# Linear attention and a low-rank mixer on one core: part of one batch's first product by Strassen's algorithm, one cast shared by two engines, a weight load gated later

## The chip, the cores and the metric

One core of a Trainium2 chip runs the whole program. The metric is the device time of one execution in microseconds (us); lower is better. The kernel before took 290.35 us (median of 3 runs, 290.05 to 291.34).

The engines are called as the profile calls them: PE (matrix products), PEld (its weight loads), DVE and ACT (elementwise work), POOL (elementwise work, and issue of one kind of DMA), SP (issue of the other kind). DMAs that POOL issues run in the queue that the profile names q0 software_dynamic, those of SP in q1 hardware_dynamic; both are served by the same 16 DMA engines.

## The reference

There are 8 batches, 8 heads, 576 positions, head width 64, model width 512. First comes attention without softmax, then a mixer:

```python
phi(x) = concat(relu(x) * cos_w, relu(x) * sin_w)        # 64 -> 128 features
kv  = einsum('bhsf,bhsd->bhfd', phi(k), v)
num = einsum('bhsf,bhfd->bhsd', phi(q), kv)
den = einsum('bhsf,bhf->bhs', phi(q), sum_s phi(k)) + 1e-6
x   = num / den                                          # as [8, 576, 512]
u   = x + (x^T @ U @ V)^T                                # U [576, 32], V [32, 576]
out = u + relu(u @ w_ch1) @ w_ch2                        # 512 -> 2048 -> 512
```

All inputs and the output are float32; the kernel computes in bf16 with float32 sums.

## The kernel before

**Tiling.** A batch's 576 positions are four blocks of 128 and a tail of 64; the tails of two batches share one block. A batch's first product (u times w1, 2048 hidden columns) is laid out in 16 blocks `j` of 128 hidden columns; plain, each block takes four matmuls of 128x512 (`g1_main`, L702 to L719) and an eviction with relu on ACT (L717). The second product (hidden times w2) gives the batch's 512 output columns.

**Strassen.** In batches 3 to 6 (`MIXED`, L815) half of the first product's blocks go by Strassen's algorithm: for `m` in (0, 2), the blocks 4m to 4m+3 take seven parts of four 128x256 matmuls each (`g1_part`, L620; matmuls L653), and the blocks 4m+4 to 4m+7, named s4 to s7, are plain ones laid between the parts. The parts need sums and differences of blocks of w1 (`w1_form`, tile `sa`, DVE, L591) and of u^T (`uT_form`, tile `tb`, DVE, L608). Parts 1, 6, 5 and 3 add up one after the other in one bank of PSUM (`al_ps`) and ACT reads it after each (L114 to tile `pw`, or L687); parts 2, 7 and 4 go to banks called `be_ps`, and DVE adds the `pw` copy to each (L678). Part 4 adds onto part 7's bank, after DVE has read that. The relu of these blocks is made by DVE (L675), or for the batches in `RELU_A` by ACT two slots later (L670). The second product of batches 1 to 7 goes by Strassen as a whole (`w_part`, matmuls L892, sums of hidden blocks by `hid_form`, L857).

**Order.** The order of all work is written out by hand. A list of slots holds PE's units in order, batch after batch; `todo` and `beside` hang other work (loads, casts, the attention of a later batch) on slot numbers, and each engine runs its instructions in the order in which they were written. In a slot, PE's own unit comes first, then what hangs on it. `starts[b]` is the slot at which batch b's first product begins; starts[2] is slot 70. The tail's second product of the first pair (`g2_tail`, L796) is in the slots 66 to 69.

**The start.** SP loads q, k and v of batch 0 (v in four DMAs: two for heads 0 to 3, two for heads 4 to 7; L74 and L80). DVE and ACT make the features of q and k, PE the transposes of q and the sums over k. Then `first_chain` (L1269) makes batch 0's x: v is cast to bf16 (tile `v0`, DVE, L116: heads 0 and 1, heads 2 and 3, then heads 4 to 7 in one instruction); the product of k and v is made for heads 0 to 3 (L353) and for heads 4 to 7 (`kv_unit`, L341); the reciprocals of the denominators (`rec`, L429 and L430) and the normalisation (L1240, DVE, nine instructions, and L1263, ACT) follow, then u^T and the first product. POOL loads w1 in four quarters and w2 in four quarters (L102, L108). Each of these loads waits for a mark: a one-element copy by POOL that reads something which must be done first. The first quarter of w1 waits for `q_tl` (L1352), its other quarters for `q_tlT` (L1358), w2 for the transposed q of batch 1 (L1380). In the same way SP's loads of batch 1 stand behind small DMAs that read `k_p` (L1354) and `z_sb` (L1361).

**Banks of PSUM.** `G3` is three banks that are used in turn, `T1` one bank, `OA` and `OB` one each, which are there only from slot starts[3] - 2 on.

**SP in the steady state.** SP issues the loads of the next batch and the transposes of q (`qtr_dma`, L408 and L413) and of u (`utr_dma`, L535 and L541), in order; each waits in SP's queue for its data. Batch 7's transposes of q stand ahead of batch 6's transposes of u.

Of the kernel before, what the change touches and what calls it, by code (L numbers as in the profile page):

```python
# [10 lines left out]
FP32 = mybir.dt.float32  # L11
# [6 lines left out]
def kernel(  # L18
# [11 lines left out]
    nc = tc.nc  # L30

    B = 8
    H = 8
# [3 lines left out]
    P = 128  # L37
    DM = 512
# [207 lines left out]
    X1S = ("x", 1)  # L246
# [20 lines left out]
    def bank(shape, dt, tag, bufs, name):  # L267
        if tag == "x":
            return ps.tile([P, 2, 512], FP32, tag="X", bufs=1, name=name)[:, 0, 0 : shape[1]]
        if tag in ("oA", "oB"):  # L270
            return ps_rest[1].tile(shape, dt, tag=tag, bufs=bufs, name=name)
        if tag == "O":
            t = ps_rest[2].tile([P, 2, 512], FP32, tag=tag, bufs=bufs, name=name)
            return t if len(shape) == 3 else t[:, 0, 0 : shape[1]]
        return ps.tile(shape, dt, tag=tag, bufs=bufs, name=name)
# [331 lines left out]
        )[n]  # L607
        V_.tensor_tensor(out=t[:, n], in0=a, in1=b_, op=ALU.subtract)  # L608

    RELU_A = (4, 6)  # L610
    relus = []

    def late_relus():
# [6 lines left out]
    def g1_part(b, m, part):  # L620
        if b not in hid:
            hid[b] = pool.tile([P, NJ, 512], BF16, tag="hid", bufs=1, name="hid")
        last = b == B - 1
        if b not in pw:
            pw[b] = [
                pool.tile([P, 3, 512], FP32, tag=tag, bufs=1, name="pw")
                for tag in ("pw", "k_p")[: 1 + last]
            ]
        ks = slice(2 * m, 2 * m + 2)

        def s_of(n):
            return sa[m % 2][:, m // 2, n]

        lhs, rhs = {
            1: lambda: (w1_block(0, 0, ks), uT_block(b, 0, 0)),
            2: lambda: (w1_block(0, 1, ks), uT_block(b, 1, 0)),
            3: lambda: (s_of(3), uT_block(b, 1, 1)),
            4: lambda: (w1_block(1, 1, ks), tb[b][:, 3]),
            5: lambda: (s_of(0), tb[b][:, 0]),
            6: lambda: (s_of(1), tb[b][:, 1]),  # L640
            7: lambda: (s_of(2), tb[b][:, 2]),
        }[part]()
        if part == 1:
            g_al[b, m] = bank([P, DM], FP32, *((OA, OB, T1)[m % 3] if last else T1), "al_ps")
        elif part in (2, 7):
            tg = (X1S, G3) if last else (G3, OA)
            g_be[b, m, part] = bank([P, DM], FP32, *tg[part == 7], "be_ps")
        t = g_al[b, m] if part in (1, 3, 5, 6) else g_be[b, m, 2 if part == 2 else 7]
        opens = part in (1, 2, 7)
        res = t.rearrange("p (k n) -> p k n", k=2)  # L650
        for k_ in range(2):
            for d in range(2):
                nc.tensor.matmul(  # L653
                    out=res[:, k_, :], lhsT=lhs[:, d, k_, :], rhs=rhs[:, d, :],
                    start=(opens and k_ == 0 and d == 0), stop=(k_ == 1 and d == 1),
                    skip_group_check=not opens,
                )
        p_, w_, y_ = (
            pw[b][m % 2 if last else 0][:, i].rearrange("p (k n) -> p k n", k=2)
            for i in range(3)  # L660
        )

        def block(i, r):
            return hid_block(b, i, r, ks)

        def relu(o):
            if b in RELU_A:
                relus.append([
                    2,
                    lambda: nc.scalar.activation(  # L670
                        out=o, in_=o, func=AF.Relu, bias=0.0, scale=1.0
                    ),
                ])
                return
            V_.tensor_scalar(out=o, in0=o, scalar1=0.0, scalar2=None, op0=ALU.max)  # L675

        def add(o, x):
            V_.tensor_tensor(out=o, in0=x, in1=res, op=ALU.add)  # L678

        if part == 1:  # L680
            cast(A_, p_, res)
        elif part == 6:
            cast(A_, w_, res)
        elif part == 5:
            cast(A_, y_, res)
        elif part == 3:
            nc.scalar.activation(  # L687
                out=block(0, 1), in_=res, func=AF.Relu, bias=0.0, scale=1.0
            )
        elif part == 2:  # L690
            add(block(0, 0), p_)
            relu(block(0, 0))
        elif part == 7:
            add(block(1, 1), y_)
            relu(block(1, 1))
        else:
            add(block(1, 0), w_)
            relu(block(1, 0))
# [96 lines left out]

    def g2_tail(pr, part):  # L796
        if part == 0:
            o_ps[pr] = bank([P, DM], FP32, *(OB if pr else T1), "ot_ps")
        o = o_ps[pr]
        for j in range(part * 4, part * 4 + 4):  # L800
            nc.tensor.matmul(  # L801
                out=o, lhsT=hid_tl[pr][:, j, :], rhs=w2_bf[:, j, :],
                start=(j == 0), stop=(j == NJ - 1),
            )
        if part < 3:
            return
        o_s = pool.tile([P, DM], FP32, tag="o_tl", bufs=1, name="o_tl")
        nc.vector.tensor_tensor(out=o_s, in0=u_tl[pr], in1=o, op=ALU.add)
        for i in range(2):
            store_eng(2 * pr).dma_start(  # L810
                out=out[2 * pr + i].rearrange("(m k) n -> m k n", k=9)[:, 4],
                in_=o_s[i * TS : i * TS + TS, :],
            )

    MIXED = {3: (0, 2), 4: (0, 2), 5: (0, 2), 6: (0, 2)}  # L815
    FULL = [b for b, ms in MIXED.items() if 2 in ms]
    HD = DM // 2
    KB = NJ // 2
# [223 lines left out]
    def lay(units, in_second):  # L1042
        slots.extend(units)
        second.extend([in_second] * len(units))

    HALF = ("1", "s4", "6 2", "s5", "5 7", "s6", "3", "s7 4")

    def first_units(b):
        starts[b] = len(slots)

        def unit(names, m):
            def go():
                for n in names:
                    if n[0] == "s":
                        g1_main(b, 4 * m + int(n[1]))
                    else:
                        g1_part(b, m, int(n))

            return go

        for m in (0, 2):
            if m in MIXED.get(b, ()):
                lay([unit(n.split(), m) for n in HALF], False)
            else:
                lay([lambda j=j: g1_main(b, j) for j in range(4 * m, 4 * m + 8)], False)
        for i in range(4 * (0 < b)):
            n = 12 + 2 * i if b == 1 else (9, 11, 17, 18)[i] if b in MIXED else 8 + i
            beside.setdefault(starts[b] + n, []).append(
                lambda i=i: hid_form(b, (1, 2, 4, 3)[i], 0)
            )  # L1070
# [58 lines left out]
    def attention_plan(b):  # L1129
# [22 lines left out]
        else:  # L1152
# [6 lines left out]
                        put(F + s_, feature, *ops.pop(0), eng)  # L1159
            V0 = starts[b - 2] + 9 if b > 3 else F + 1  # L1160
            at_q, at_load = (F + 7, F + 8, F + 8) if late else (F + 5, F + 7, F + 7), (F + 8, F + (16 if late else 14), V0 + (8 if late else 5))
            if b == 6:
                at_q, at_load = (F + 7, F + 12, F + 12), (F + 12, F + 16, V0 + 8)
            if b == 3:
# [7 lines left out]
            if late:  # L1172
                kv_at, x_at = G + 3, [G + i for i in (5, 8, 13, 16, 18)]
            elif b - 1 in FULL:
                kv_at, x_at = G + 1, [G + i for i in ODDX]
            elif b - 1 in MIXED:
                kv_at, x_at = G + 1, [G + i for i in X5]
            a_at = x_at[4] + (3 if b in (4, 6) else 2)
            u_at = a_at + 1
# [89 lines left out]
    def first_chain(b, xz, z, v_ps):  # L1269
# [9 lines left out]
        cast(V_, v0[:, 0:2], vst[:, 0:2])  # L1279
        cast(V_, z_sb, z[:, :, 0])  # L1280
        cast(V_, v0[:, 2:4], vst[:, 2:4])
        cast(V_, v0[:, 4:H], vst[:, 4:H])
        qtr_evac(b, 4, A_, t_q[4])
        kv_sb[b] = pool.tile([P, H, E], BF16, tag="kv", bufs=2, name="kv")
        acc = bank([P, 4, D], FP32, *G3, "kv_ps")
# [2 lines left out]
        kv0_mm(b, acc, (2, 3))  # L1288
        cast(A_, V_bf, v_ps.rearrange("r (c p) -> r c p", c=4))
        cast(A_, kv_sb[b][:, 0:4, 0:D], acc)  # L1290
        den_mm(b, d, (3, 4))
        recip(rec, d[:, :, :, 0])
        x0 = [xh_mm(b, c, 0, *G3) for c in ORD[0:2]]
# [55 lines left out]
        z_mm(0, c, z)  # L1349
    qtr_evac(0, 3, A_, t_q[3])  # L1350

    G_.tensor_copy(out=mark[0:1], in_=q_tl[0:1, 0, 0:1])  # L1352
    w1_load(0)
    nc.sync.dma_start(out=mark2, in_=k_p[0][0:1, 0, 0, 0:1])  # L1354
    load_odd(qst, q, 1)
    load_even(qst, q, 1)
    first_chain(0, xz, z, v_ps)
# [77 lines left out]
    def put(at, thunk):  # L1435
        todo.setdefault(at, []).append(thunk)
# [2 lines left out]
    s6 = starts[B - 2]  # L1439
    for n in range(4):  # L1440
        for m in (0, 2):
            put(starts[2] + (-4, -3, -1, 1)[n], lambda n=n, m=m: w1_form(n, m))
            put(
                (s6 + (1, 2, 3, 4)[n], starts[B - 1] + (-3, -1, 1, 3)[n])[m // 2],
                lambda n=n, m=m: w1_form(n, m + 1),
            )
        for b in MIXED:
            put(starts[b] + (-3, -2, 0, 2)[n], lambda b=b, n=n: uT_form(b, n))
        put(starts[B - 1] + (-2, -1, 0, 2)[n], lambda n=n: uT_form(B - 1, n))
        put(starts[B - 1] + len(LAST) + 5 + 2 * n, lambda n=n: tl_form(n))  # L1450
# [43 lines left out]
```

## Time and profile before

| what | value |
|---|---|
| median of 3 runs | 290.35 us (290.05 to 291.34) |
| the profiled execution's own time | 290.51 us |
| its span (first to last instruction) | 288.7 us |
| PE busy | 98% of the span, 3110 matmuls |
| DVE, ACT, POOL busy | 76%, 61%, 25% of the span |
| DMA | 53.32 MB, 185 GB/s over the span |
| granted clock of PE | 0.999 |

The span is the time from the first to the last instruction in the trace; the own time of the same execution is 1.8 us longer. Times inside the trace count from the span's start. A matmul's record in the trace is longer than the distance to the next one, since matmuls are pipelined: a group of four 128x512 is recorded as 1.03 us and holds PE for 0.86.

### The profile page before, as it was taken

Reading aid. Unit: us, or ns where it says so; the run is one execution under the profiler, and the core shown is the slowest. Engines: PE = TensorE matmul, PEld = TensorE weight load, DVE = VectorE, ACT = ScalarE, POOL = GpSimd, SP = SyncE. Lnnn points to the kernel's source line nnn. Section 1 sums busy time; section 2 is a strip of 40 time slices with the busy share of each in tenths; the row PEclk is TensorE's granted clock in tenths of the full one; section 3 lists DMA queues with packets and bytes.
Section 4 is the critical chain, followed back from the end, with each engine's and each line's share of the span. In section 5 each row is a group of like instructions: output and inputs, shape, how many; then the busy total and the mean of one; then the engine's idle time right before and its main releaser. Section 6 shows DMA issues by size and latency. Waiting matters only on the chain.

```text
span 288.7 us, 7553 instructions
## 1 busy us (share of the span) xinstructions
PE 283.0 (98%) x3110; PEld 209.6 (73%) x3110; DVE 218.9 (76%) x446; ACT 175.5 (61%) x308; POOL 70.9 (25%) x111
## 2 busy tenths in 40 slices
PE   8999999999999999999999999999999999999995
PEld 6776455545887646886887667876888778899884
DVE  4979738887886677558895388958898689689864
ACT  2955661476687366986587488776795772177110
POOL 8340600040045304441006500351006000400140
PEclk9999999999999999999999999999999999999999
DMA  6999999999959898899829993599978200620023
GB/s 197 339 284 253 287 209 259 276 211 176 299 156 177 226 360 174 212 275 299 218 38 185 298 290 105 61 213 207 260 141 147 93 1 8 150 83 2 0 88 132
DMA packets 85447, 53.32 MB, mean 185 GB/s; under 512 B 53990, under 2 KB 83078, under 8 KB 85414
## 3 DMA queue, kind: packets, MB, share of 16 engines
q1 hardware_dynamic: 78998, 41.62, 60.0%
q0 software_dynamic: 6272, 11.17, 16.2%
q8 instruction: 24, 0.39, 0.6%
q10 hardware_dynamic: 144, 0.07, 0.1%
q14 instruction: 9, 0.07, 0.1%
HBM read 36.86 MB, written 9.44 MB: 160 GB/s over the span
## 4 chain that ended last, share of the span: by engine, by line
PE 92%; DMA 3%; DVE 2%; SPq 1%; issue 0%; DVEq 0%
PE w_ps L892 30%; PE g_ps L710 24%; PE al_ps L653 7%; PE be_ps L653 5%; PE gt_ps L741 5%; PE o_ps L781 5%; DMA vst<-in_v_dram 3%; PE x_ps L439 3%; PE kv_ps L364 3%; PE ot_ps L801 2%; PE ot_ps L994 2%; PE a_ps L465 1%; PE va_ps L495 1%; PE t_ps L382 1%; PE g_ps L727 0%; PE va_ps L518 0%
## 5 line engine op out<-in xcount | busy, mean ns | idle before, releaser
L710 PE MATMUL g_ps<-uT,w_bf 128*128 128x512 bf16 x314 | 77.0, 379 | 0.0
L717 ACT ACTIVATE hid<-g_ps 128x512 bf16<-128x512 f32 x80 | 47.4, 597 | 31.8 <-PE g_ps L710 26.6
L912 POOL TENSOR_TENSOR o_sb<-o_sb,u_bf 128x512 f32<-128x512 f32 x21 | 26.2, 1259 | 111.9 <-DVE o_sb L912 111.9
L710 PEld LDWEIGHTS <-w_bf 128*128 128x128 bf16 x314 | 29.1, 98 | 25.9
L892 PEld LDWEIGHTS <-hid 128*128 128x128 bf16 x448 | 43.1, 98 | 5.6 <-DVE hid L857 0.2
L678 DVE TENSOR_TENSOR hid<-pw,be_ps 128x512 bf16<-128x512 f32 x36 | 24.7, 686 | 17.0 <-PE be_ps L653 10.0
L892 PEld LDWEIGHTS <-S 128*128 128x128 bf16 x336 | 32.2, 98 | 4.5
L114 ACT ACTIVATE pw<-al_ps 128x512 f32<-128x512 f32 x36 | 21.3, 595 | 16.5 <-PE al_ps L653 8.9
L892 PE MATMUL w_ps<-T,hid 128*128 128x256 bf16 x224 | 27.9, 273 | 0.0
L892 PE MATMUL w_ps<-w_bf,hid 128*128 128x256 bf16 x224 | 27.6, 273 | 0.0
L892 PE MATMUL w_ps<-T,S 128*128 128x256 bf16 x224 | 27.1, 273 | 0.0
L114 ACT ACTIVATE o_sb<-w_ps 128x512 f32<-128x512 f32 x21 | 12.5, 597 | 20.5 <-PE w_ps L892 14.1
L912 DVE TENSOR_TENSOR o_sb<-o_sb,w_ps 128x512 f32<-128x512 f32 x21 | 14.3, 683 | 12.0 <-ACT o_sb L114 7.6
L506 DVE TENSOR_TENSOR u_bf<-x_bf,va_ps 128x1024 bf16<-128x1024 bf16 (+1 forms) x20 | 19.5, 998 | 3.4 <-PE va_ps L495 2.7
L653 PEld LDWEIGHTS <-sa 128*128 128x128 bf16 x192 | 17.7, 98 | 4.0 <-issue 0.2
L449 DVE TENSOR_TENSOR x_bf<-x_ps,rec 128x512 bf16<-128x512 f32 x28 | 19.3, 691 | 1.0
L305 ACT ACTIVATE k_p<-kst,sinw 128x512 bf16<-128x512 f32 x26 | 17.8, 713 | 0.1
L653 PEld LDWEIGHTS <-w_bf 128*128 128x128 bf16 x144 | 14.0, 98 | 3.5
L116 POOL CAST v_ext<-vst 128x512 bf16<-128x512 f32 x24 | 14.7, 652 | 7.1 <-issue 3.2
L741 PE MATMUL gt_ps<-uT_tl,w_bf 128*128 128x128 bf16 x256 | 16.4, 219 | 0.0
L781 PE MATMUL o_ps<-w_bf,hid 128*128 128x512 bf16 x64 | 15.6, 379 | 0.0
L741 PEld LDWEIGHTS <-w_bf 128*128 128x128 bf16 x256 | 15.0, 98 | 0.4
(191 smaller groups left out, 499.9 us busy)
## 6 DMA issues: line engine op xcount, KB each, us to landing
qst<-in_q_dram SPq DMA_DIRECT2D x14, 512.0 KB, 6.8
kst<-in_k_dram SPq DMA_DIRECT2D x14, 512.0 KB, 8.6
vst<-in_v_dram SPq DMA_DIRECT2D x12, 512.0 KB, 8.4
out_dram<-o_sb POOLq DMA_DIRECT2D x12, 512.0 KB, 5.4
w_bf<-in_moe_w_ch_dram POOLq DMA_DIRECT2D x8, 512.0 KB, 10.9
out_dram<-o_sb SPq DMA_DIRECT2D x4, 512.0 KB, 3.0
qst<-in_q_dram SPq DMA_DIRECT2D x2, 640.0 KB, 5.9
kst<-in_k_dram SPq DMA_DIRECT2D x2, 640.0 KB, 13.6
```

The source lines that it names most:

```text
L114: nc.scalar.activation(out=o, in_=i, func=AF.Copy, bias=0.0, scale=1.0)
L305: nc.scalar.activation(out=o, in_=i, func=AF.Relu, bias=0.0, scale=w)
L449: nc.vector.tensor_tensor(out=x_of(b, c, rows).rearrange("p (g i d) -> p g i d", g=2, d=D), in0=view[:, :, :, 0:D], in1=rec[rows].unsqueez ...
L506: nc.vector.tensor_tensor(out=u_bf[b][:, d0 : d0 + n], in0=x_bf[b].rearrange("p c (d n) -> p d c n", n=P)[:, d0 : d0 + n], in1=t.rearrange ...
L653: nc.tensor.matmul(out=res[:, k_, :], lhsT=lhs[:, d, k_, :], rhs=rhs[:, d, :], start=(opens and k_ == 0 and d == 0), stop=(k_ == 1 and d = ...
L678: V_.tensor_tensor(out=o, in0=x, in1=res, op=ALU.add)
L710: nc.tensor.matmul(out=g_ps.rearrange("p (c t) -> p c t", c=4), lhsT=w1_bf[:, d, j * P : j * P + P], rhs=uT[b][:, d, :, :], start=(d == 0) ...
L717: nc.scalar.activation(out=hid[b][:, j, :], in_=g_ps, func=AF.Relu, bias=0.0, scale=1.0)
L741: nc.tensor.matmul(out=g_ps[:, jj, :], lhsT=w1_bf[:, d, j * P : j * P + P], rhs=uT_tl[pr][:, d, :], start=(d == 0), stop=(d == 3),)
L781: nc.tensor.matmul(out=o, lhsT=hid[0][:, j, cc * P : cc * P + P], rhs=w2_bf[:, j, :], start=(j == 0), stop=(j == NJ - 1),)
L892: nc.tensor.matmul(out=res[:, g, :], lhsT=lhs[:, k_, g * P : g * P + P], rhs=rhs[:, k_, :], start=(opens and k_ == 0 and g == 0), stop=(k_ ...
L912: eng.tensor_tensor(out=o_, in0=x, in1=y, op=ALU.add)
```

## The change

It has four parts.

1. **Batch 2's first quarter by Strassen.** `MIXED` gets `2: (0,)`: blocks 0 to 3 of batch 2 go by the seven parts, blocks 4 to 7 lie between them, blocks 8 to 15 stay plain. Its relus go to ACT (`RELU_A`). The last unit is written "4 s7" and not "s7 4". Part 7's bank is one of `G3`, as `OA` is not there yet; the first pair's `g2_tail` moves from `T1` to `G3`, as `T1` holds `al_ps`. The w1 sums are made earlier: those for m = 0 in slots 66 to 69 and those for m = 2 in slots 62 to 65 (both were in 66, 67, 69 and 71). The hidden sums of batch 2 move one slot later.
2. **The cast of v.** Heads 4 and 5 stay with DVE; heads 6 and 7 are cast by ACT, behind its eviction of the product for heads 0 to 3.
3. **Gates at the start.** w1's first quarter waits for the first block of k's features (`k_p`) in place of `q_tl`; SP's load of batch 1's q waits for the second block of `k_p` in place of the first.
4. **u^T ahead of q^T.** Two of batch 7's transposes of q are put four slots later; on SP, batch 6's first two transposes of u now come ahead of them.

```diff
-    RELU_A = (4, 6)
+    RELU_A = (2, 4, 6)
...
-            tg = (X1S, G3) if last else (G3, OA)
+            tg = (X1S, G3) if last else (G3, OA if b > 2 else G3)
...
-            o_ps[pr] = bank([P, DM], FP32, *(OB if pr else T1), "ot_ps")
+            o_ps[pr] = bank([P, DM], FP32, *(OB if pr else G3), "ot_ps")
...
-    MIXED = {3: (0, 2), 4: (0, 2), 5: (0, 2), 6: (0, 2)}
+    MIXED = {2: (0,), 3: (0, 2), 4: (0, 2), 5: (0, 2), 6: (0, 2)}
...
     HALF = ("1", "s4", "6 2", "s5", "5 7", "s6", "3", "s7 4")
+    HALF2 = ("1", "s4", "6 2", "s5", "5 7", "s6", "3", "4 s7")
...
-                lay([unit(n.split(), m) for n in HALF], False)
+                lay([unit(n.split(), m) for n in (HALF if b > 2 else HALF2)], False)
...
-            n = 12 + 2 * i if b == 1 else (9, 11, 17, 18)[i] if b in MIXED else 8 + i
+            n = 12 + 2 * i if b == 1 else (9, 11, 17, 18)[i] if b in MIXED and b > 2 else 8 + i + (b == 2)
...
+            if b == 7:
+                at_q = (F + 5, F + 11, F + 11)
...
-            elif b - 1 in MIXED:
+            elif b > 3 and b - 1 in MIXED:
                 kv_at, x_at = G + 1, [G + i for i in X5]
...
-        cast(V_, v0[:, 4:H], vst[:, 4:H])
+        cast(V_, v0[:, 4:6], vst[:, 4:6])
...
         cast(A_, kv_sb[b][:, 0:4, 0:D], acc)
+        cast(A_, v0[:, 6:H], vst[:, 6:H])
...
-    G_.tensor_copy(out=mark[0:1], in_=q_tl[0:1, 0, 0:1])
+    G_.tensor_copy(out=mark[0:1], in_=k_p[0][0:1, 0, 0, 0:1])
     w1_load(0)
-    nc.sync.dma_start(out=mark2, in_=k_p[0][0:1, 0, 0, 0:1])
+    nc.sync.dma_start(out=mark2, in_=k_p[0][0:1, 1, 0, 0:1])
...
-            put(starts[2] + (-4, -3, -1, 1)[n], lambda n=n, m=m: w1_form(n, m))
+            put(starts[2] + (n - 4 if m == 0 else n - 8), lambda n=n, m=m: w1_form(n, m))
```

## The prediction

> **What bounds the kernel now.** I read the busy shares first, then PE's waits, then the chain of work that ended last.
>
> ```profile
> PE 283.0 (98%) x3110; PEld 209.6 (73%) x3110; DVE 218.9 (76%) x446; ACT 175.5 (61%) x308; POOL 70.9 (25%) x111
> ```
>
> ```profile
> PE w_ps L202 <- DVE zero L125: 1.2, 1, 1.2
> PE t_ps L394 <- ACT q_p L305: 0.4, 1, 0.4
> PE kv_ps L341 <- DVE v L116: 0.4, 1, 0.4
> ```
>
> PE is busy for 98% of the span, and the list of its waits is complete with three: all lie in the first 17 us. From 21.7 us to 285.4 us PE never stands still. So only two things can shorten the kernel: fewer PE columns, or an earlier start of that dense stretch; and anything that makes PE wait inside it costs its full length. The chain shows what holds the start:
>
> ```profile
> 6.06 9.86 DMA vst<-in_v_dram
> 16.01 0.83 DVE v L116
> 17.90 0.67 DVE x_bf L1240 x2
> ...
> 32.88 6.15 PE g_ps L710 x28
> 39.02 0.86 PE o_ps L781 x4
> ```
>
> v's last DMA lands at 15.92, DVE casts heads 4 to 7, and only then makes the reciprocals:
>
> ```profile
> 16.01 0.83 DVE L116 CAST v<-vst 128x1280 bf16<-128x1280 f32 x1 [1.11 <-DMA vst<-in_v_dram]
> 16.75 0.19 DVE L429 TENSOR_SCALAR rec<-xz 128x40 f32<-128x40 f32 x1
> 16.98 0.40 DVE L430 RECIPROCAL rec<-rec 128x40 f32<-128x40 f32 x1
> 17.48 0.42 DVE L1240 TENSOR_TENSOR x_tl<-xh_ps,rec 64x256 bf16<-64x256 f32 x1
> ```
>
> From 17.48 DVE normalises without a break to 20.55; the rest up to the first product at 21.70 hangs on that.
>
> **Part 1, batch 2's first quarter.** In the chain four 128x512 take 0.86 us ("PE g_ps L710 x4") and four 128x256 take 0.44 ("PE al_ps L653 x4"). Removed: four blocks, 4 x 0.865 = 3.46. Added: seven parts, 7 x 0.437 = 3.06. PE saves 0.40 us.
> The Trainium skill (TensorE: Matmul & The Clock Gate, Back-to-back issue gap) speaks against this: it gives a sustained 131 ns for 512 columns and 81 for 128. As an estimate from that page (98 ns for 256 on a straight line), 28 x 98 = 2.74 against 16 x 131 = 2.10, a loss of 0.64. The chain's 216 and 109 ns don't agree with it.
>
> The new waits have to be checked one by one against what is queued on DVE and ACT. Added on ACT: three copies, one relu from PSUM (0.60 each) and three relus (0.62), less four evictions (0.60): +1.9 us. Added on DVE: four forms (0.42 to 0.49) and three adds (0.69): +3.9 us, while six w1 forms (0.42) leave for slots before 96 us. In 96 to 112 us DVE is busy for 12.3 of 16 us and ACT for 8.8, so both still fit, but DVE with little to spare. Local order decides. The tightest spot is part 4: it adds onto part 7's bank, which DVE must have read, and DVE's add needs ACT's copy of part 5, which stands behind the eviction of s5 and the relu of part 2. Batch 4 already runs just this sequence:
>
> ```profile
> 164.81 0.60 ACT L717 ACTIVATE hid<-g_ps 128x512 bf16<-128x512 f32 x1 [0.63 <-PE g_ps L710]
> 165.31 0.62 ACT L670 ACTIVATE hid<-hid 128x512 bf16<-128x512 bf16 x1
> 165.83 0.59 ACT L114 ACTIVATE pw<-al_ps 128x512 f32<-128x512 f32 x1
> ```
>
> There PE issues s5 at 163.75 and DVE's add starts at 166.45 and ends at 167.14, 3.39 us after s5. In batch 2 PE wants part 4 after s5 (0.865), part 5 and part 7 (0.87), a product of x (0.26), s6 (0.865) and part 3 (0.44): 3.30 us. Batch 4 has s7's 0.86 in between ("s7 4"); batch 2 has not ("4 s7"). So PE waits some 0.15 us (bounds 0, if ACT runs a little ahead, and 0.4). Behind it, the bank for block 9 needs DVE's add of part 4: that add waits for the normalisation of x before it and ends about 0.4 us before PE wants the bank; no wait. **Net: -0.25 us** (0 to -0.40). The earlier w1 forms stand in DVE's order at 87 to 97 us, where it idles 1.7 us at 86.3 and 1.7 at 93.6; u^T's second half has landed at 91.5, a microsecond before its form. `g2_tail` in G3 takes a bank that is read by 96.8 and wanted again at about 98.6.
>
> **Part 2 and the first gate.** DVE's cast becomes 0.48 (the row of its 128x640 casts). The other half goes to ACT, which evicts from 15.63 to 16.02, so it runs from 16.0 to about 16.75 (between ACT's 0.59 for 512 columns and 1.00 for 1024). PE makes heads 4 and 5 first and reaches head 6 at about 16.8, so ACT's half is hardly waited for. The reciprocal then waits for the last denominators, which PE ends at 16.19: it starts at 16.25 in place of 16.75, **0.50 us earlier**, if v lands by 15.7. If v stays at 15.92, the gain is 0.33.
> Does it land earlier? Between 14.0 and 15.7 us the queues show:
>
> ```profile
> q0 software_dynamic: 325, 0.33, 117.1%
> q1 hardware_dynamic: 11, 0.01, 3.9%
> ```
>
> q1's packets here are v's last ten, on one DMA engine that a 16 KB instruction packet (1.14 us from 13.62) had held up. They start at 14.75 and share the engine with w1's first quarter: the first five take 0.14 us each, later ones 0.055. Issued at 10.40, w1's first packets came at 13.65, 3.25 us later. The new gate (k's first block, done at about 11.8 in place of 10.2) moves the issue to 11.96 and the packets to about 15.2; the ten then take 0.55 us and end at 15.30 in place of 15.72. So v lands at 15.5 and the 0.50 holds.
> The Trainium skill (DMA: Bandwidth & Descriptors, Specifications) gives a DMA issued by GpSimd about 1 us to its first byte; by an estimate from it w1 would come at 13.8, still meet v's tail, and the gain would be 0.33. The 3.25 us of the trace disagrees.
> w1's first quarter landed at 18.69 and is wanted at 21.2; even 1.6 us later it is in time. Batch 1's q landed at 22.16 and its user comes at 21.9 now, but those features have 0.8 us before PE needs them.
>
> **What is late next.** This decides how much of the 0.50 stays. The next data that PE needs are w2's first quarter, at 38.86. The rows of that DMA and of PE:
>
> ```profile
> L108 POOL DMA_DIRECT2D w_bf<-in_moe_w_ch_dram x1: 747/747/747, 30.6 to 30.6; - x1
> ...
> DMA to landing us min/median/max: 8.2/8.2/8.2
> ```
>
> ```profile
> 38.86 1.03 PE L781 MATMUL o_ps<-w_bf,hid 128*128 128x512 bf16 x4
> ```
>
> Issued at 30.60, landed at 38.81: 0.05 us before PE's first use. PE will be there at 38.36. The last share comes from the slowest DMA engine (the other fifteen are done by 37.8), and that engine has had packets of one queue or the other without a break since 13.6 us; the change moves the same bytes. If it is only work that counts, the landing stays at 38.8 and PE keeps 0.05 of its 0.50. If the engine's order improves by as much as v's tail (0.41), PE keeps 0.46. I take 0.20, nearer to the unmoved end, because the bytes are the same: **-0.20 us** (-0.05 to -0.46).
>
> **Second gate and part 4.** Batch 1's q is issued 0.42 us later, but its packets began at 16.17, right after v's tail, so the tail sets them: 0. On SP, batch 7's transposes of q move behind two waits for batch 6's u, whose adds DVE ends at 214.4 and 215.6: their second half then lands some 7 us later than now, near 226, and PE uses it from 230.3 on. u^T is issued about 1 us earlier and landed at 221.1 before, a microsecond ahead of its use at 222, without a wait: 0 either way.
>
> **Sum.** -0.25 - 0.20 = -0.45 on the profiled execution's 290.51 gives 290.06. That execution lies 0.16 above the median, so **289.9 us**.
>
> **Rivals.**
> - *The w2 gate gives way* (chance 0.22): its landing moves with the start, and part 4 does not wait. -0.90, 289.45 us. For it: the laggard engine shared badly at 15 us. Against: its unbroken work.
> - *POOL's queue is late as a whole* (0.10, the slower side): w1's first quarter is 1.56 us later, w1's other quarters and w2 stand behind it, and w2's first quarter lands at 40.37. PE waits 1.51, less 0.25: 291.6 us. It decides once the first quarter's last packet on the slow engine, 18.57 now, comes after about 20.9, when the second quarter's began there. Against: those 2.3 us of slack.
> - *Batch 2's stage stalls* (0.11): DVE's chain (add of part 7, normalisation, add of part 4) runs a half to one us late and PE waits at part 4 or block 9. It eats the 0.40 and up to 0.6 more: 290.2 to 290.8 us.
> - *Half-width matmuls cost what their records say* (0.02): 273 and 379 ns are the mean records; 28 x 0.273 less 16 x 0.379 is +1.58, with the start's 0.20 291.7 us. The chain's distances refute it.
>
> **How the numbers follow.** Forecast 0.55 (289.6 to 290.3). The range 289.1 to 291.0 takes in the first and third rival and the half us by which medians of few runs stray (the three shown span 1.3); it leaves out the second and fourth. Half a per cent (1.45 us) is about what a measurement can tell: below 288.9 only if the w2 gate gives way and more comes with it, 0.06; above 291.8 only if POOL's queue is later still, 0.06; the rest, 0.88, is within.
>
> **What would show it.** Right: `rec` at about 16.25 and the first product at 21.2; then a PE wait for a w2 load just before 38.8; a wait of 0.1 to 0.2 us at part 4 near 101.7; no other. Wrong: PE reaching 38.4 and going on; a first product still at 21.7; PE waiting for w1 near 26 or 31 us; waits of over 0.3 us near 102 to 104.

## The result, and the profile after

The changed kernel takes **291.53 us** (median of 16 runs, 290.85 to 292.86); the kernel before took 290.81 in the same 16 rounds (290.05 to 292.78). The ratio is **1.0033, 95% interval 1.0019 to 1.0046**: slower by 0.33%, about 1 us. That is within the half per cent that the prediction took for the least a measurement can tell, but on the other side of 1, above its range, and clear of noise. The lowest runs say it most plainly: no run of the changed kernel in these rounds came below 290.85, while before reaches 290.05.

The profiled execution of the changed kernel is one of its longest: 292.52 us, span 290.7. So the profile shows the loss and some bad luck besides, and the experiments have to tell the two apart. First PE's waits in it; the columns are the total, the number and the longest, in us:

```profile
PE w_ps L202 <- DVE zero L125: 1.2, 1, 1.2
PE t_ps L382 <- ACT q_tl L305: 1.1, 1, 1.1
PE x_ps L439 <- DVE kv L116: 0.5, 1, 0.5
PE kv_ps L364 <- DVE k_p L307: 0.2, 1, 0.2
PE t_ps L394 <- POOL U_bf L116: 0.2, 1, 0.2
PE o_ps L781 <- DMA w_bf<-in_moe_w_ch_dram: 0.2, 1, 0.2
```

Before, the three waits all lay ahead of the dense stretch. Now four lie inside it: `q_tl` at 24.7 us, w2 at 40.0, and `kv_ps` and `x_ps` at 95 to 98.6. The sum closes: the first product starts 0.45 earlier, batch 2 takes 0.40 fewer (both were forecast), and PE loses 1.27 at `q_tl`, 0.33 at w2, 0.36 and 0.67 in batch 2's stage and 0.14 at part 4, counted as the distance between two matmuls less what the first of them takes. 2.77 less 0.85 is 1.92 of the 2.01 us by which this execution is longer than the one profiled before.

**The start went as forecast.** In DVE's timeline of the changed kernel (start, us, work):

```profile
15.61 0.49 DVE L116 CAST v<-vst 128x640 bf16<-128x640 f32 x1 [0.56 <-DMA vst<-in_v_dram]
16.17 0.20 DVE L429 TENSOR_SCALAR rec<-xz 128x40 f32<-128x40 f32 x1
```

The reciprocal starts at 16.17, not 16.75; v landed at 15.52. In PE's timeline the first product follows at 21.25, and 3.4 us later comes the first new wait:

```profile
21.25 1.47 PE L727 MATMUL g_ps<-uT,w_bf 128*128 128x512 bf16 x6
...
24.69 0.51 PE L382 MATMUL t_ps<-ident,q_tl 128*128 128x128 bf16 x6 [1.11 <-ACT q_tl L305]
```

What ACT and DVE waited for stands in DVE's row, batch 1's q:

```profile
23.86 0.48 DVE L307 TENSOR_SCALAR q_tl<-qst,cosw 128x512 bf16<-128x512 f32 x1 [1.81 <-DMA qst<-in_q_dram]
```

**The DMA engines stood half idle.** A row of the table by windows gives the stretch and its length, the busy time of PE, PEld, DVE, ACT and POOL (with the number of instructions), PE's granted clock, the DMA engines' busy share (1 and more is full) and GB/s; over 1 us, GB/s are KB. 14 to 15 us, before:

```profile
14.00:15.00 1.00, 1.00 (x37) 0.96 (x37) 0.75 (x3) 1.00 (x2) 0.00 (x0) 1.00 1.20 200
```

and in the changed kernel:

```profile
14.00:15.00 1.00, 0.91 (x30) 0.91 (x31) 0.86 (x3) 1.00 (x3) 0.00 (x0) 1.00 0.51 52
```

By 14.0 us all but the last four of v's packets have begun. Before, w1's packets ran among them from 13.41 on, 0.096 to 0.098 us each; now the quarter is issued at 12.13, its first packets begin at 13.74, twelve of them take 0.4 to 1.2 us, and the stream flows only from 14.7. Almost nothing else runs in between: batch 1's q, issued at 13.04, began its packets at 17.04, as w1's quarter ran out (15.90 before). The bytes are not made up by 30 us: from 8 us to there the engines move 6.10 MB where they had moved 6.34, and at the 250 KB a us of the stretch from 20 to 30 the 0.24 MB are, as an estimate, 1.0 us. w2's first quarter is issued and lands (POOL's timeline, then the last line of the view of this one DMA):

```profile
31.43 0.74 POOL L108 DMA_DIRECT2D w_bf<-in_moe_w_ch_dram  x1 [0.28 <-issue]
...
DMA to landing us min/median/max: 8.5/8.5/8.5
```

at 39.98 us (38.81 before), and PE, which was there 0.33 earlier even after the wait for `q_tl`, goes on at 40.02.

**Batch 2's stage.** DVE's rows of a w1 sum and of k's features take 0.42 and 0.47 us otherwise. Here:

```profile
89.78 1.23 DVE L591 TENSOR_TENSOR sa<-w_bf 128x512 bf16<-128x512 bf16 x1
90.93 1.38 DVE L307 TENSOR_SCALAR k_p<-kst,sinw 128x512 bf16<-128x512 f32 x1
...
92.83 1.35 DVE L591 TENSOR_TENSOR sa<-sa,w_bf 128x512 bf16<-128x512 bf16 x1
```

POOL's timeline at that time:

```profile
89.57 2.45 POOL L912 TENSOR_TENSOR o_sb<-o_sb,u_bf 128x512 f32<-128x512 f32 x2
...
92.74 1.15 POOL L912 TENSOR_TENSOR o_sb<-o_sb,u_bf 128x512 f32<-128x512 f32 x1
```

Each stretched row lies beside one of POOL's sums. The Trainium skill (SBUF — State Buffer, SBUF: two separate sides) says that DVE and POOL share a pair of ports by an exclusive lock, held for a whole instruction; the rows agree: 0.8 to 0.9 us more where the two overlap. POOL's sums are late because its casts of batch 3's v ahead of them waited for the DMA until 87.9 us; its odd part landed at 86.3 (82.6 before), issued at 76.5 (74.4), behind transposes and loads that SP issued later than before.

### The profile page after: what moved, and what is told of

It reads as the page before. It is cut to its first block, busy times and chain, and to the rows that moved or that the text cites. A ratio compares the mean times of both kernels' runs of the same rounds, so it can differ in the third digit from the quotient of the medians.

```text
span 290.7 us, 7592 instructions
## 1 busy us (share of the span) xinstructions
PE 283.6 (98%) x3122; PEld 210.8 (73%) x3122; DVE 223.6 (77%) x453; ACT 177.3 (61%) x312; POOL 69.1 (24%) x111
## 3 DMA queue, kind: packets, MB, share of 16 engines
HBM read 36.86 MB, written 9.44 MB: 159 GB/s over the span
## 4 chain that ended last, share of the span: by engine, by line
PE 83%; DMA 9%; DVE 4%; ACT 1%; issue 1%; POOL 0%; ACTq 0%; DVEq 0%; POOLq 0%
PE w_ps L892 28%; PE g_ps L710 19%; PE al_ps L653 8%; PE be_ps L653 6%; PE gt_ps L741 5%; PE o_ps L781 5%; DMA qst<-in_q_dram 3%; PE x_ps L439 3%; DMA w_bf<-in_moe_w_ch_dram 3%; DMA kst<-in_k_dram 3%; PE ot_ps L994 2%; PE kv_ps L364 2%; DVE sa L591 1%; PE ot_ps L801 1%; PE a_ps L465 1%
## 5 line engine op out<-in xcount | busy, mean ns | idle before, releaser
L710 PE MATMUL g_ps<-uT,w_bf 128*128 128x512 bf16 x298 | 73.5, 379 | 0.0
L717 ACT ACTIVATE hid<-g_ps 128x512 bf16<-128x512 f32 x76 | 45.0, 597 | 26.1 <-PE g_ps L710 25.8
L710 PEld LDWEIGHTS <-w_bf 128*128 128x128 bf16 x298 | 27.5, 98 | 23.8
L678 DVE TENSOR_TENSOR hid<-pw,be_ps 128x512 bf16<-128x512 f32 x39 | 26.7, 685 | 17.6 <-PE be_ps L653 10.0
L114 ACT ACTIVATE pw<-al_ps 128x512 f32<-128x512 f32 x39 | 23.1, 595 | 21.2 <-PE al_ps L653 13.7
L653 PEld LDWEIGHTS <-sa 128*128 128x128 bf16 x208 | 19.3, 98 | 4.9 <-issue 0.3
L653 PEld LDWEIGHTS <-w_bf 128*128 128x128 bf16 x156 | 15.2, 98 | 4.0 <-issue 0.2
L116 POOL CAST v_ext<-vst 128x512 bf16<-128x512 f32 x24 | 14.0, 622 | 8.8 <-DMA vst<-in_v_dram 5.5
L781 PE MATMUL o_ps<-w_bf,hid 128*128 128x512 bf16 x64 | 15.6, 379 | 0.2 <-DMA w_bf<-in_moe_w_ch_dram 0.2
L653 PE MATMUL al_ps<-tb,sa 128*128 128x256 bf16 x104 | 15.6, 272 | 0.0
## 6 DMA issues: line engine op xcount, KB each, us to landing
kst<-in_k_dram SPq DMA_DIRECT2D x2, 640.0 KB, 15.8
```

Source lines behind the costliest of these rows:

```text
L114: nc.scalar.activation(out=o, in_=i, func=AF.Copy, bias=0.0, scale=1.0)
L653: nc.tensor.matmul(out=res[:, k_, :], lhsT=lhs[:, d, k_, :], rhs=rhs[:, d, :], start=(opens and k_ == 0 and d == 0), stop=(k_ == 1 and d = ...
L710: nc.tensor.matmul(out=g_ps.rearrange("p (c t) -> p c t", c=4), lhsT=w1_bf[:, d, j * P : j * P + P], rhs=uT[b][:, d, :, :], start=(d == 0) ...
L717: nc.scalar.activation(out=hid[b][:, j, :], in_=g_ps, func=AF.Relu, bias=0.0, scale=1.0)
L781: nc.tensor.matmul(out=o, lhsT=hid[0][:, j, cc * P : cc * P + P], rhs=w2_bf[:, j, :], start=(j == 0), stop=(j == NJ - 1),)
```

## The experiments

Ratios are to the kernel before, run on the same chip between the others; its median lay between 290.29 and 290.49 us each time. First each half of the change alone.

**e1: the product alone** (part 1, with the w1 sums moved; start and transposes as before).

```diff
-    MIXED = {3: (0, 2), 4: (0, 2), 5: (0, 2), 6: (0, 2)}
+    MIXED = {2: (0,), 3: (0, 2), 4: (0, 2), 5: (0, 2), 6: (0, 2)}
...
-            put(starts[2] + (-4, -3, -1, 1)[n], lambda n=n, m=m: w1_form(n, m))
+            put(starts[2] + (n - 4 if m == 0 else n - 8), lambda n=n, m=m: w1_form(n, m))
```

> Only part 1 of the change (batch 2's quarter by Strassen, with its w1 forms in slots 62 to 69). Theory A, the loss is made in batch 2's stage: PE saves 0.40 us and waits 0.36 for the last feature of batch 3's k, 0.67 for the eviction of kv and 0.14 at part 4, so this kernel is slower than before by about 0.8 us. Rival B, the loss is made at the start: this kernel is faster by 0.1 to 0.4 us.

Measured: 290.74 us, 1.0011 (0.9993 to 1.0028). In its profile PE has no wait at 95 to 99 us, 0.14 at part 4, 0.24 at an `x_ps` near 236, and 0.86 at w2's first quarter, which landed at 39.41 with the old gate: one DMA engine was late there, and the other fifteen had their shares through by 37.62. It neither wins nor loses measurably.

**e2: the start alone** (parts 2 and 3).

```diff
-        cast(V_, v0[:, 4:H], vst[:, 4:H])
+        cast(V_, v0[:, 4:6], vst[:, 4:6])
...
+        cast(A_, v0[:, 6:H], vst[:, 6:H])
...
-    G_.tensor_copy(out=mark[0:1], in_=q_tl[0:1, 0, 0:1])
+    G_.tensor_copy(out=mark[0:1], in_=k_p[0][0:1, 0, 0, 0:1])
...
-    nc.sync.dma_start(out=mark2, in_=k_p[0][0:1, 0, 0, 0:1])
+    nc.sync.dma_start(out=mark2, in_=k_p[0][0:1, 1, 0, 0:1])
```

> Only the cast shared by two engines and the two later gates. Theory A: the first product begins 0.45 us earlier, and what the later loads take back (PE waits for batch 1's q, then for w2's first quarter) leaves 0 to +0.3 us against before. Rival B: slower by 0.8 us or more, with the 1.1 us wait for batch 1's q seen in the changed kernel's profile.

Measured: 291.42 us, 1.0037 (1.0017 to 1.0057), no run below 290.92. First product at 21.25, then 0.91 us lost at w2's first quarter, which landed at 39.38. The loss is the start's.

**e3: the cast alone.**

```diff
-        cast(V_, v0[:, 4:H], vst[:, 4:H])
+        cast(V_, v0[:, 4:6], vst[:, 4:6])
...
+        cast(A_, v0[:, 6:H], vst[:, 6:H])
```

> Only the cast shared by two engines; both gates as before. v lands at about 15.9 as before. The reciprocal starts at about 16.4 in place of 16.75, so the first product begins 0.3 us earlier. If w2's first quarter is a fixed gate (landing at 38.8), PE then waits about 0.25 us there and the time stays within 0.1 us of before; if the gate moves with the start, 0.3 us faster. Batch 1's q lands at 22.2 as before and PE does not wait for it.

Measured: 290.87 us, 1.0021 (0.9996 to 1.0047); the runs lie in two heaps, 290.1 to 290.3 and 290.7 and up. First product at 21.09, w2 landed at 38.42. The cast doesn't make the loss that every run of e2 has: its lowest run is 290.13.

**e4: the w1 sums alone** (moved, on the kernel before, without the product they are moved for).

```diff
-            put(starts[2] + (-4, -3, -1, 1)[n], lambda n=n, m=m: w1_form(n, m))
+            put(starts[2] + (n - 4 if m == 0 else n - 8), lambda n=n, m=m: w1_form(n, m))
```

> The kernel before with only the w1 forms moved (those for m = 2 to slots 62 to 65, those for m = 0 to slots 66 to 69). Theory A1, DVE's forms and features are held up while POOL runs its adds of u: DVE's rows of 0.42 and 0.48 us become 1.2 to 1.4 us between 88 and 94 us, PE waits 0.2 to 0.4 us for batch 3's k features, and the eviction of kv is late; slower by 0.3 to 0.9 us. Rival A2, the stage is late because of the added forms of u^T and adds: no stretched rows and no wait, within 0.1 us of before.

Measured: 290.40 us, 1.0001 (0.9988 to 1.0014). Its profile (291.34 us, one of its longest) has the stretched DVE rows again, 1.38 and 1.37 us beside POOL's sums at 89.3 and 92.6, and PE loses 0.57 at `kv_ps`; there too batch 3's v had landed late, at 85.9. Other profiles have single stretched rows (e1 one of 1.38 us at 89.5) and no wait of PE. So the stall is real, it was seen in the two profiles where v landed near 86 and in no other, and the median does not show it.

Now the two gates, one by one.

**e5: w1's gate alone.**

```diff
-    G_.tensor_copy(out=mark[0:1], in_=q_tl[0:1, 0, 0:1])
+    G_.tensor_copy(out=mark[0:1], in_=k_p[0][0:1, 0, 0, 0:1])
```

> Before with one line of the change: w1's first quarter waits for k's first features instead of q's; nothing else. Theory A (a hole in the stream of the DMA engines): the 16 engines are busy from 8 us until w2's first quarter has landed; the later gate leaves them 60 to 90% busy at 13 to 15 us, and all that follows comes later. Expected: w2's first quarter at 39.3 to 40 us (38.81 in the profile of before), PE waiting for it by 0.5 to 1 us, 291.1 to 291.6 us. Rival (the split cast or the later load of batch 1's q makes the loss): as before, 290.4 us, w2's first quarter at 38.8.

Measured: 291.62 us, **1.0042 (1.0026 to 1.0058)**, no run below 290.94: this one line costs as much as the whole change. The window of 14 to 15 us and PE at w2:

```profile
14.00:15.00 1.00, 0.89 (x25) 0.76 (x25) 1.00 (x3) 1.00 (x2) 0.00 (x0) 1.00 0.44 28
```

```profile
39.94 1.02 PE L781 MATMUL o_ps<-w_bf,hid 128*128 128x512 bf16 x4 [0.74 <-DMA w_bf<-in_moe_w_ch_dram]
```

**e6: all of the change but this line**; against the changed kernel:

```diff
-    G_.tensor_copy(out=mark[0:1], in_=k_p[0][0:1, 0, 0, 0:1])
+    G_.tensor_copy(out=mark[0:1], in_=q_tl[0:1, 0, 0:1])
```

> The changed kernel with w1's first quarter gated as before; the product, the split cast, batch 1's q one block later and the order of the transposes stay changed. Theory A: no hole, w2's first quarter at 38.4 to 39.0 us, no wait of PE for q_tl at 23 us, 290.0 to 290.5 us. Rival (the loss hangs on batch 1's q, or on batch 2's product): 291.2 us or more.

Measured: 290.47 us, 0.9990 (0.9975 to 1.0006), lowest 289.94. The hole is gone, and w2's first quarter lands at 38.45:

```profile
14.00:15.00 1.00, 1.00 (x40) 0.96 (x37) 0.56 (x2) 1.00 (x3) 0.00 (x0) 1.00 1.23 205
```

With e5 this settles which line it is: without it the loss is gone, and with it alone it is all there.

**e7: the hole filled with batch 1's q** (the changed kernel, SP's gate on `q_tl`).

```diff
-    nc.sync.dma_start(out=mark2, in_=k_p[0][0:1, 1, 0, 0:1])
+    nc.sync.dma_start(out=mark2, in_=q_tl[0:1, 0, 0:1])
```

> The changed kernel with the two gates exchanged: w1's first quarter waits for k's first features as in the change, but SP's load of batch 1's q waits for q_tl, so that it is issued near 10.4 us and its packets can come right behind v's last ones. Theory A: the hole at 13 to 15 us is filled by q's packets, batch 1's q lands some 3 us earlier (no wait for q_tl), w1's first quarter lands near 19.5 us, before its use at 21.2, and w2's first quarter at 38.8 or a little earlier: 289.9 to 290.4 us. Rival (w1's first quarter passes its own delay down POOL's queue): w2's first quarter at 39.5 or later, 291.2 us or more. A third outcome, PE waiting for w1's first quarter at 21.2, would say that q's packets took its place: 0.5 us or more there.

Measured: 291.13 us, 1.0015 (1.0003 to 1.0028). The hole is filled and w2's first quarter lands at 38.87 with w1 gated late all the same, so it wasn't the gate's delay passed down POOL's queue that made w2 late. But the time was lost again elsewhere, by the third outcome:

```profile
14.00:15.00 1.00, 0.93 (x31) 0.92 (x32) 0.86 (x3) 1.00 (x3) 0.00 (x0) 1.00 1.07 354
```

```profile
22.20 1.47 PE L727 MATMUL g_ps<-uT,w_bf 128*128 128x512 bf16 x6 [0.88 <-DMA w_bf<-in_moe_w_ch_dram]
```

w1's packets came only as q's ran out, from 16.50 us, and the quarter landed at 22.15. KB moved by all engines in each us, as the windows give it:

| us | before | changed | e5 | e6 | e7 |
|---|---|---|---|---|---|
| 13 to 14 | 304 | 220 | 219 | 278 | 354 |
| 14 to 15 | 200 | 52 | 28 | 205 | 354 |
| 15 to 16 | 209 | 205 | 166 | 214 | 364 |
| 16 to 17 | 348 | 202 | 210 | 362 | 318 |
| all from 8 to 30 | 6344 | 6103 | 6039 | 6301 | 6441 |

**e8: the product with room** (before, with part 1; the last unit as in the other batches, and the w1 sums for m = 2 in a slot at 68 us where DVE and POOL idle).

```diff
-    HALF2 = ("1", "s4", "6 2", "s5", "5 7", "s6", "3", "4 s7")
+    HALF2 = ("1", "s4", "6 2", "s5", "5 7", "s6", "3", "s7 4")
...
-            put(starts[2] + (n - 4 if m == 0 else n - 8), lambda n=n, m=m: w1_form(n, m))
+            put(starts[2] + n - 4 if m == 0 else 42, lambda n=n, m=m: w1_form(n, m))
```

> Before with batch 2's first quarter by Strassen as in the change, but with room: the last unit is s7 and then part 4 (so that DVE's add of part 7 has 0.86 us more), and the four w1 sums for m = 2 are made in slot 42, where DVE and POOL idle, so that none of them stands in DVE's order beside POOL's sums at 87 to 97 us. If four half-width matmuls cost 0.437 us as in the chain and only the waits ate it: no wait of PE at 95 to 105 us, and 0.40 less than before, 290.0 us. If the half-width parts save nothing: 290.4 with no wait; with waits still there the room was not what they lacked.

Measured: 290.18 us, 0.9999 (0.9987 to 1.0012); lowest 289.80, profiled 289.98. No wait at part 4, none at 95 to 105 us. The saving can be read off PE's timeline between two points with the same work but for the product. Before:

```profile
95.05 1.03 PE L801 MATMUL ot_ps<-w_bf,hid_tl 128*128 128x512 bf16 x4
...
112.41 1.80 PE L892 MATMUL w_ps<-w_bf,hid 128*128 128x256 bf16 x15
```

and in e8:

```profile
94.62 1.03 PE L801 MATMUL ot_ps<-w_bf,hid_tl 128*128 128x512 bf16 x4
...
111.58 2.67 PE L892 MATMUL w_ps<-w_bf,hid 128*128 128x256 bf16 x23
```

17.36 against 16.96: **0.40 us**, as worked out. But 0.23 of it is lost again at an `x_ps` near 234.5 us, as in the profiles of e1, e6, e7 and e9.

Three more: **e9: e6 with e8's room**, **e10: the changed kernel with e8's room** (both have the edit of e8; e9 has the old gate of w1 besides), and **e11: the changed kernel once more**, with no edit.

```diff
-    HALF2 = ("1", "s4", "6 2", "s5", "5 7", "s6", "3", "4 s7")
+    HALF2 = ("1", "s4", "6 2", "s5", "5 7", "s6", "3", "s7 4")
...
+            put(starts[2] + n - 4 if m == 0 else 42, lambda n=n, m=m: w1_form(n, m))
```

> All of the change but the later gate of w1's first quarter, and batch 2's product with room (s7 before part 4, the w1 sums for m = 2 in slot 42). If the gains add: 0.40 of the product less the 0.24 that PE lost again near 234 us with each Strassen version but the changed kernel's own execution, and 0.2 to 0.4 of the start as far as w2's first quarter (38.1 to 38.5 us) lets it: 290.0 us, 0.4 to 0.5 less than before in the same job. If PE's arrival at w2 is all that counts at the start, the split cast adds nothing: 290.2.

Measured: 290.33 us, 0.9994 (0.9971 to 1.0018), lowest 289.72. Not told apart from before: the gains expected don't show in the median.

> The changed kernel with both of its gates, but batch 2's product with room. Theory (the loss of the changed kernel is the w1 gate's, and the waits at 95 to 98 us that its profiled execution shows come only where batch 3's v lands late): 0.15 to 0.3 us below the changed kernel, 291.1 to 291.3, still slower than before. Rival (the waits in batch 2's stage carry a good part of the loss in most executions): 0.5 to 1.0 us below the changed kernel, 290.5 to 290.9.

Measured: 291.47 us, 1.0029 (1.0013 to 1.0045); no better than e11, which falls against the rival, and not the 0.15 to 0.3 below it that the theory gave. The stalls in batch 2's stage carry no part of the loss that the median shows. In its profile w2 landed at 40.79 and PE lost 0.96 at `q_tl`.

> The changed kernel once more, beside the other two on one chip and for a second profiled execution. Theory: 291.3 to 291.6 us; w2's first quarter at 39.3 us or later, since the hole in the DMA stream is there in every execution; the waits for q_tl at 23 us and in batch 2's stage are smaller than in the first profile or absent, as they hang on single packets. Rival: the same waits at 23 and 95 to 98 us again, so that they are part of the change and not of that execution.

Measured: 291.33 us, 1.0027 (1.0012 to 1.0042). The second profile of the changed kernel has no wait at 23 us and none at 95 to 99, but w2 at 39.43 and 0.57 lost there. So w2's late landing comes with the change in both of its profiles; the other two waits come with the execution.

**e12: the changed kernel with less to load** (v of heads 4 to 7 of batch 1 is left out).

```diff
-    for h0 in (0, 4):
-        load_odd(vst, v, 1, h0, h0 + 4)
-        load_even(vst, v, 1, h0, h0 + 4)
+    load_odd(vst, v, 1, 0, 4)
+    load_even(vst, v, 1, 0, 4)
```

> The changed kernel, all its gates kept, but batch 1's v of heads 4 to 7 isn't loaded (batch 0's values stay in its place), so that 0.59 MB less stand before w2's first quarter in the stream of the DMA engines, some 2 us at the 250 KB a us of that stretch. Theory (the later gate costs only through the DMA stream, by way of w2's first quarter): w2's first quarter lands at 37.5 to 38.3 us in spite of the gate, PE keeps the start it gained, and the loss turns round: 289.8 to 290.3 us, below before. Rival (the loss of the changed kernel is made elsewhere: batch 2's stage, the order of the transposes, POOL's queue by itself): 291.2 us or more, with w2 in time.

Measured: 290.76 us, 1.0019 (1.0004 to 1.0034). w2 landed at 38.34 and PE had no wait for it, as the theory has it, but the time lies between the two forecasts: about half of the loss stays. The theory of w2 alone isn't borne out. Its one profile can't say what the rest is: it began 0.44 us later than before (first product at 22.14), as k came late in it.

**e13 to e15: without the even half of batch 1's q as well**, in the changed kernel (e13), in the kernel before as control (e14), and in the control with w1's gate alone (e15).

```diff
     load_odd(qst, q, 1)
-    load_even(qst, q, 1)
```

> The changed kernel without two loads of batch 1: v of heads 4 to 7, as in the run before, and the even half of q (batch 0's values stay in both places). Theory (the rest of the loss is batch 1's q, which the later gate pushes from 22.2 to between 22.6 and 24.7 us in the profiles, so that PE waits for q_tl in part of the executions): 289.8 to 290.3 us, and below the control, the kernel before without the same loads, by 0.1 to 0.5. Rival (the rest is in the start itself or behind 40 us): 290.6 to 290.9 us, 0.3 or more above the control.

> The control: the kernel before, without the same two loads (v of heads 4 to 7 and the even half of q of batch 1). It was held by neither before, so 290.2 to 290.5 us, as the kernel before; if it falls clearly below, the loads bound the kernel before as well.

> The control with w1's first quarter gated later, the one line that cost 1.2 us with all loads in place. Theory (the gate costs only through what comes later in the DMA stream, that is batch 1's q and w2's first quarter): nothing left, within 0.3 us of the control. Rival (the gate costs by itself, by way of w1 or of POOL's queue): 0.6 us or more above the control.

Measured: e13 290.67 us, 1.0007 (0.9988 to 1.0025), lowest 289.76, profiled 289.97; e14 290.09 us, 0.9989 (0.9975 to 1.0004), lowest 289.76, profiled 289.76; e15 290.44 us, 0.9999 (0.9979 to 1.0020), lowest 289.81, profiled 289.81. With both loads gone the gate costs 0.05 us between the lowest runs and between the profiles; with all loads in place the lowest runs lie 0.90 apart (290.94 against 290.04). That speaks for a cost by way of what comes later in the DMA stream, w2 and q, and not for one of the gate's own. The medians don't show it as plainly: e15 lies 0.35 above e14, just past the 0.3 of the expectation, e13 0.58 above, and the intervals of all three overlap. Each has some runs at 290.8 to 292; what holds those is open, and with it how much of the gate's cost goes by way of w2 and q.

All profiles beside each other; gate is w1's, and e12 to e15 load less:

| | gate | v landed | first product | w2 landed | PE lost at w2 | own time |
|---|---|---|---|---|---|---|
| before | old | 15.92 | 21.70 | 38.81 | 0 | 290.51 |
| e1 | old | 14.53 | 21.32 | 39.41 | 0.86 | 291.13 |
| e3 (split cast) | old | 15.62 | 21.09 | 38.42 | 0.21 | 290.13 |
| e4 | old | 15.61 | 21.39 | 39.00 | 0.49 | 291.34 |
| e6 (split cast) | old | 15.56 | 21.01 | 38.45 | 0.20 | 290.19 |
| e8 | old | 14.24 | 21.27 | 38.12 | 0 | 289.98 |
| e9 (split cast) | old | 15.59 | 21.88 | 38.98 | 0 | 290.62 |
| changed (split cast) | new | 15.52 | 21.25 | 39.98 | 0.33 | 292.52 |
| e2 (split cast) | new | 14.31 | 21.25 | 39.38 | 0.91 | 291.07 |
| e5 | new | 15.03 | 21.84 | 39.90 | 0.90 | 291.64 |
| e10 (split cast) | new | 15.42 | 22.36 | 40.79 | 0.34 | 292.17 |
| e11 (split cast) | new | 15.98 | 21.74 | 39.43 | 0.57 | 291.04 |
| e12 (split cast) | new | 15.26 | 22.14 | 38.34 | 0 | 291.04 |

With all loads w2's first quarter lands at 38.12 to 39.41 with the old gate (mean of seven 38.74) and at 39.38 to 40.79 with the new one (mean of five 39.90); in e7, with the hole filled, at 38.87. The means lie 1.2 us apart, which fits the missing 0.24 MB (changed) and 0.30 MB (e5): 1.0 and 1.2 us by the same estimate. A landing is that of the last of sixteen shares, one for each engine, and e1 shows how far a single engine can stray. The middle of the sixteen shares says it more cleanly: 36.4 to 36.8 us in six of the seven profiles with the old gate (37.9 in e9, where k came late), 37.0 in e7, and 38.0 to 38.9 in the five with the new gate.

## Why the prediction was wrong, step by step

**The step that failed is the w2 gate**, the term of -0.20 us in the part "What is late next": "that engine has had packets of one queue or the other without a break since 13.6 us; the change moves the same bytes. If it is only work that counts, the landing stays at 38.8." The bytes are the same, but the change itself made the break. The prediction moved w1's first packets from 13.65 to about 15.2, asked what that does to v's last ten packets on one engine, and did not ask what the other fifteen would do meanwhile. From 14.0 to 15.0 us all sixteen moved 52 KB where they had moved 200. From 16 us up to w2 the stream was full in each stretch (busy share 1.13 to 1.17), so the lost time came out at its end: w2 landed 1.2 us later, where the prediction had it stay or come up to 0.41 earlier. It was not the slow engine alone: of w2's sixteen shares fifteen landed between 36.3 and 37.8 us before, and between 37.7 and 39.1 now. The term of -0.20 (bounds -0.05 to -0.46) measured +1.0 in e2, the start alone.

**Its packet times** are 0.24 us too late by the clock of the profile's other times. In the profile before, w1's first packets begin at 13.41, not 13.65, so they came 3.0 us after the issue and not 3.25; v's tail begins at 14.51 and batch 1's q at 15.90. In the changed kernel w1's first packets began at 13.74, 1.6 us after the issue, and the flow at 14.7. The prediction's second estimate, 13.8, which it set aside, was the nearer one for the first packets. v landed at 15.52 all the same, but not as worked out: one packet of its data was left after 14.0, not ten, and in e2, with the same start, v landed at 14.31.

**The rival "POOL's queue is late as a whole"** gave the sign and nearly the time, 291.6 us, but by luck: its mechanism is another, and so its condition was wrong. It was to decide only if w1's first quarter ended late on the slow engine; there it ended earlier than before (18.00 against 18.69), on the other fifteen engines later (by 18.0 against 16.8), and w2 was late. e7 tells the two apart: the same late gate, w2 on time. Its "against" (2.3 us of slack) was true of w1 and had no bearing on w2.

**"Batch 1's q ... 0.8 us before PE needs them"** was wrong in two of the six profiles with the change's kind of start: `q_tl` waited until 23.9 us in the changed kernel and 24.7 in e10, and PE lost 1.27 and 0.96; in e2, e5, e11 and e12 it was in time. Behind it, "the tail sets them: 0" failed as well: q's packets start behind w1's first quarter, at 17.04 in place of 15.90. It was so before, too: in e8 v had landed by 14.24, and q's packets still flowed only from 15.8.

**The start: -0.50 forecast, -0.45 in the profile, but less in truth.** `rec` at 16.25 (16.17) and the first product at 21.2 (21.25) were met, but the term was measured against an execution in which v came late. In others of the same code v lands at 14.2 to 14.5, and the cast isn't on the path at all. DVE in e8, which casts as before:

```profile
14.38 1.22 DVE L116 CAST v<-vst 128x640 bf16<-128x640 f32 x2
16.31 0.20 DVE L429 TENSOR_SCALAR rec<-xz 128x40 f32<-128x40 f32 x1 [0.71 <-PE xz L1225]
```

v is cast by 15.6 and `rec` waits for PE's denominators: first product at 21.27, with the old cast. With a late v the split cast gains 0.3 to 0.7 (21.01 and 21.09 against 21.39 and 21.70). In a third kind k is late, and nothing about v matters; DVE in e10:

```profile
12.37 1.28 DVE L307 TENSOR_SCALAR k_p<-kst,cosw 128x512 bf16<-128x512 f32 x3 [1.02 <-DMA kst<-in_k_dram]
```

(11.34 before). e5, e9, e10 and e12 were profiled in that kind, with either gate, and start at 21.8 to 22.4. Why k's load comes late in some executions wasn't settled; it may be a good part of what scatters the runs.

**Part 1: -0.40 right to the hundredth, the wait at part 4 right** (0.15 forecast, 0.14 measured in each kernel with "4 s7", and none with "s7 4"). That it is 0.14 is in part luck: the working, 3.39 less 3.30, gives 0.09, and the prediction doesn't say where the rest of its 0.15 comes from. "The earlier w1 forms stand in DVE's order ... where it idles" is right when batch 3's v lands near 82 us and wrong when it lands near 86, as POOL's sums then come to lie on them; no median showed the difference. The sustained figures of the Trainium skill that spoke against it (TensorE: Matmul & The Clock Gate, Back-to-back issue gap) would, by the prediction's estimate, have made it 0.64 us longer; the 0.40 us less disagree. That the gain doesn't show in e8's ratio either (0.9999) is in part the 0.23 us lost again at 234 us; why DVE's work ahead of it starts 0.35 later against PE than it did before I could not settle.

**Part 4: 0**, as forecast: no wait of PE for u^T or q^T there in any profile. It wasn't run alone.

**The range** took in no loss at w2: the failed step's bounds were both gains, and the rival that had a loss there was left out.

No version ran measurably below before: e6, e8 and e9 have 0.9990, 0.9999 and 0.9994, all with 1 inside their intervals.

## What to carry to other kernels

Before you delay a load, look at what the DMA engines do in the time it leaves: where they are full up to a load that PE waits for, a hole of a microsecond comes out at that load, whatever the delayed one's own slack is. Ask it of all 16 engines, not only of the slow one, and count bytes moved up to the deadline rather than each load's landing. And take a term that rests on one late packet from several executions: here the 0.5 us were there only in those where v was late.

## What the runs showed of the hardware

- From POOL's issue of a load to the flow of its packets passed 2.6 us in the changed kernel (12.13 to 14.7) and 3.1 before (10.40 to 13.5). In the changed kernel, where the engines were running out of work, the first packets came 1.6 us after the issue, but took up to 1.2 us each, the later ones 0.098. Before, where the engines were busy until the packets came, the first took 0.096. So a gate on such a load has to open about 3 us ahead of the gap that the load is to fill.
- A queue whose packets come second isn't served at once. In e7 w1's quarter, issued at 12.11, moved nothing until 16.50 us, while q's packets ran. In every other profile q's flow began 2.3 to 2.6 us after that of w1's quarter, whether that was 2.2 us after q's own issue (e9) or 4.3 (e5). Later, at 22 to 25 us, both queues move some 120 to 130 KB a us side by side. The Trainium skill (DMA: Bandwidth & Descriptors, Queues, rings and completion order) lets each DMA engine go round between the queues that it has work for, by packets. That agrees with the later stretch; whether it agrees with these starts depends on when the second queue's packets were ready, which no trace here shows.
- The 16 engines move 350 to 390 KB a us of SP's loads, about 205 of POOL's casting loads, and 250 with both. But the profile counts a casting load by the bf16 bytes that it writes (a quarter of w1 is 512 packets of 1024 bytes). The 36.86 MB that it gives as read from HBM are reached only if the weights are counted as float32, so 205 KB written are 410 KB read. Casting loads look dear in KB as counted; by what they read they are not.
